# Layer 1 in units of one tile with two places for its middle, and layer 2's first weight scaled by halves

## The chip, the cores and the metric

The kernel runs on one core of one Trainium2 chip. The metric is device time in microseconds (us) of one execution; smaller is better. The core has TensorE (PE, matmuls; PEld are its weight loads), VectorE (DVE), ScalarE (ACT), GpSimd (POOL), SyncE (SP, which issues the DMAs here) and 16 DMA engines.

## What is computed

Masked attention, then two layers of the same shape, on 1536 tokens (2 batches of 768) of width 512:

```python
q_assign = argmax(q_n @ c_n.T)           # 16 clusters per head, k likewise
scores = where(q_assign[:, None] == k_assign[None, :], q @ k.T / 8, -1e9)
x = softmax(scores) @ v                  # 2 batches, 8 heads, 768 x 64, then (1536, 512)
h = x @ w_in; x = (h * cos(h)) @ w_out   # layer 1: 512 -> 2048 -> 512
h = x @ w2_in; out = (h * sigmoid(h)) @ w2_out   # layer 2, same sizes
```

The weights come as 64-bit floats.

## The kernel before

Every product is made of float16 halves: each operand is scaled by a power of two and split into a high and a low part, and three products (high by high, high by low, low by high) are summed in PSUM. So a weight is first unpacked from 64 bits to float32 (`conv`, L685 to L720: three VectorE passes per chunk of 128 x 512, or two and an addition on GpSimd), then a scale is found, then it is split (`split`, L752).

A tile is 128 tokens of one batch, six to a batch. The two batches are cut into `UNITS` (L26) of one or two tiles: one, one, two, two, and then two, two, two. For every unit `attention` (L884) makes, for each tile and each of eight heads, the scores (L905, 128 x 768 in PSUM), their maximum (L915), two one-column factors (L919, L920), the exponential (L934), the halves of it (L941, L948), their transposition by DMA (L514), and the product with V (L958). Eight heads give x of the tile, which is scaled, halved and transposed by DMA into `xT` (L986).

Layer 1 follows a unit later. `layer1_in` (L1011) multiplies the transposed x by the first weight, 768 columns of PSUM at a time (L1034 to L1036), and takes h cos(h) by L1049 to L1058 into `gT`, in halves. `gT` holds one unit: one place in `p_g`. `layer1_out` (L1064) multiplies `gT` by the second weight (L1092 to L1094) in two passes of two blocks of 128 output columns, for there is one PSUM bank (`g2_ps`) of 512 columns, evicts them with a factor (L1099), takes the absolute maximum (L1103, by L411), and stores them to DRAM (L1107). With two tiles in a unit a matmul streams 256 columns, with one 128.

`layer2` (L1116) runs on blocks of 512 tokens. After the last attention and the last conversion of its second weight (`t_swap`) the memory of attention is given to it. It unpacks its first weight (L1128, 16 chunks, each with a sum of squares, L438), finds one scale for it from the sum over all of them (`f_scale`, L1130), splits it in eight pieces (L1140), then splits the second weight (L1151), whose float32 form lies in DRAM. For a block it finds a scale from the maxima of its units (L1169 to L1184), halves the block's x in one operation each (L1185, L1187), multiplies (L1205 to L1207), takes h sigmoid(h) by Tanh (L1215 to L1221), and multiplies by the second weight (L1236 to L1238).

What sets the order: the program is a graph of tasks. `Graph.run` (L141) goes through it once in Python before anything is issued, keeps a clock for each engine from costs written in the code, and starts at each moment the ready task with the smallest due time (`pri`) whose buffers are free. The order that comes out is the order of instructions on each engine. The due times are sums of the unit's number times 1000 and the constants in `T` (L22). They aren't times, only an order. The load of a weight chunk has its own due time, `pri - T["W_AHEAD"]` (L692). Two rules hold the stages in a fixed order: scores of unit u wait for the layer-1 matmuls of unit u - 2 (`g1_dep`, L889 and L912), and those of u wait for the last scores of u + 1 (`last_s`, L1039); likewise the exponentials and the sines (L936, L1053), so that ScalarE seldom changes its table.

In the first stage places are shared: the two halves of `xT` are staging for half of the chunks of layer 1's second weight (`p_wx`, L807 and L846), so the first x wait for all of these (`x_free`, L847 and L988). The four quarters d of that weight are staged in `gT` and in the weight's own memory (`place`, L831); d = 3 goes where d = 1 was. Their due times are `PW_OUT + PW_STEP * d`, plus the chunk (L840), which is 833 for d = 3.

```python
UNITS = [(0, 0, 1), (0, 1, 1), (0, 2, 2), (0, 4, 2), (1, 0, 2), (1, 2, 2), (1, 4, 2)]   # batch, first tile, tiles
p_x, p_g = BufPool(xT), BufPool([gT])
tms.append(add("PE", mm(n, 12), f_mm, [*xready[u], *wdep, *(last_s.get(u + 1, []) ...)], pr + i, acq=[hb], use=[xb]))
t_sc = [f_scale(0, mx0, ms, base), f_scale(1, w2_mx, w2_done, base)]
tx = add("DVE", dve(2048), lambda sx=sx: DV.scalar_tensor_tensor(
    l2["x"][:, 1], l2["xf"], sx, l2["x"][:, 0], op0=ALU.mult, op1=ALU.subtract), [th], pr, use=[xfb, xb], port=True)
```

## Time and profile before

| what | value |
|---|---|
| median of 3 runs | 816.58 us (813.89 to 818.96) |
| the profiled execution, its own time | 815.3 us |
| its span, first to last instruction | 813.6 us |
| busy: TensorE / its weight loads | 709.3 us (87%) / 483.4 us (59%) |
| busy: VectorE / ScalarE / GpSimd | 547.6 / 491.9 / 288.0 us |
| mean granted TensorE clock | 0.979 of 2.4 GHz |
| matmuls | 6744 |

Durations come from the profiled execution. Busy time is the union of an engine's instructions; a matmul's own time includes its way through the array, so the rate is read from the starts of consecutive ones. "Idle before, releaser" is the time an engine stood still ahead of an instruction, and what ended it.

### The profile page before, as it was taken

Reading aid. Unit: us, or ns where it says so; the run is one execution under the profiler, and the core shown is the slowest. Engines: PE = TensorE matmul, PEld = TensorE weight load, DVE = VectorE, ACT = ScalarE, POOL = GpSimd, SP = SyncE. Lnnn points to the kernel's source line nnn. Section 1 sums busy time; section 2 is a strip of 40 time slices with the busy share of each in tenths; the row PEclk is TensorE's granted clock in tenths of the full one; section 3 lists DMA queues with packets and bytes.
Section 4 is the critical chain, followed back from the end, with each engine's and each line's share of the span. In section 5 each row is a group of like instructions: output and inputs, shape, how many; then the busy total and the mean of one; then the engine's idle time right before and its main releaser. Section 6 shows DMA issues by size and latency. Waiting matters only on the chain.

```text
span 813.6 us, 16849 instructions
## 1 busy us (share of the span) xinstructions
PE 709.3 (87%) x6744; PEld 483.4 (59%) x6744; DVE 547.6 (67%) x1143; ACT 491.9 (60%) x767; POOL 288.0 (35%) x239
## 2 busy tenths in 40 slices
PE   2467767988879998998999999975999999999998
PEld 1344344867758876877887888862444444444443
DVE  7899988888887899698688665859860155005500
ACT  4658777788878788698488663836750155015400
POOL 3242466366675457367358540514210000000000
PEclk9999999999998999999999999996999999999999
DMA  8944399989999989959929965331401000000000
GB/s 298 308 163 143 93 222 221 218 137 192 218 184 195 255 156 188 202 134 197 212 90 199 225 194 175 105 130 53 137 27 69 27 1 0 27 27 1 0 27 26
DMA packets 233902, 111.29 MB, mean 137 GB/s; under 512 B 199520, under 2 KB 221536, under 8 KB 233824
## 3 DMA queue, kind: packets, MB, share of 16 engines
q1 hardware_dynamic: 233824, 110.23, 61.4%
q8 instruction: 52, 0.85, 0.4%
q14 instruction: 26, 0.21, 0.1%
HBM read 50.36 MB, written 10.49 MB: 75 GB/s over the span
## 4 chain that ended last, share of the span: by engine, by line
PE 41%; DVE 7%; DMA 5%; issue 2%; POOL 2%; ACT 2%; SPq 1%; POOLq 0%; DVEq 0%; ACTq 0%
PE pb L1206 5%; PE pb L1207 5%; PE pb L1205 5%; DMA gen<-gen 3%; PE xn_ps L1236 3%; PE xn_ps L1238 3%; PE g_ps L1236 3%; PE xn_ps L1237 3%; PE g_ps L1237 3%; PE g_ps L1238 3%; PE g_ps L1094 2%; PE g_ps L1093 2%; PE g_ps L1092 2%; DMA ws<-in_moe_w_in_dram 2%; POOL gen L948 1%
## 5 line engine op out<-in xcount | busy, mean ns | idle before, releaser
L948 POOL TENSOR_TENSOR gen<-e,gen 128x768 f16<-128x768 f32 x96 | 159.0, 1667 | 55.2 <-ACT gen L941 29.3
L1034 PE MATMUL pb<-xT,w 128*128 128x256 f16 (+1 forms) x448 | 111.0, 261 | 3.0 <-ACT e L934 2.7
L1092 PE MATMUL g_ps<-gT,w 128*128 128x256 f16 (+1 forms) x448 | 110.9, 259 | 2.7 <-ACT x2s L1099 2.7
L934 ACT ACTIVATE e<-pb,small 128x768 f32<-128x768 f32 x96 | 94.5, 990 | 27.6 <-DVE small L919 11.6
L1035 PE MATMUL pb<-xT,w 128*128 128x256 f16 (+1 forms) x448 | 111.0, 261 | 0.0
L1093 PE MATMUL g_ps<-gT,w 128*128 128x256 f16 (+1 forms) x448 | 110.9, 259 | 0.0
L1094 PE MATMUL g_ps<-gT,w 128*128 128x256 f16 (+1 forms) x448 | 110.9, 259 | 0.0
L1036 PE MATMUL pb<-xT,w 128*128 128x256 f16 (+1 forms) x448 | 110.8, 261 | 0.0
L915 DVE TENSOR_REDUCE small<-pb 128x1 f32<-128x768 f32 x96 | 89.7, 951 | 11.7 <-PE pb L905 11.0
L1217 DVE SCALAR_TENSOR_TENSOR e<-e,pb 128x512 f32<-128x512 f32 x48 | 32.7, 685 | 95.9 <-ACT e L1215 95.9
L1058 POOL TENSOR_TENSOR gT<-e,gT 128x768 f16<-128x768 f32 (+2 forms) x36 | 56.0, 1559 | 93.3 <-ACT gT L1057 86.2
L905 PE MATMUL pb<-kst,qst 96*128 96x512 f16 (+3 forms) x384 | 78.6, 333 | 9.5 <-ACT e L934 3.2
L958 PE MATMUL xn_ps<-vst,gen 128*128 128x64 f16 x1728 | 66.3, 195 | 21.5 <-DMA gen<-gen 20.6
L958 PEld LDWEIGHTS <-gen 128*128 128x128 f16 x1728 | 60.2, 99 | 34.2 <-DMA gen<-gen 28.9
L1206 PE MATMUL pb<-x2T,w 128*128 128x512 f16 x192 | 73.7, 384 | 6.5 <-DVE x2T L1187 6.5
L1205 PE MATMUL pb<-x2T,w 128*128 128x512 f16 x192 | 73.8, 385 | 3.7 <-ACT x2T L1185 3.7
L1207 PE MATMUL pb<-x2T,w 128*128 128x512 f16 x192 | 73.8, 384 | 0.0
L941 ACT ACTIVATE gen<-e 128x768 f16<-128x768 f32 x89 | 73.1, 841 | 0.2
L905 PEld LDWEIGHTS <-qst 128*128 128x128 f16 (+1 forms) x384 | 35.7, 99 | 29.7 <-issue 13.3
L1221 DVE SCALAR_TENSOR_TENSOR w<-e,w 128x512 f16<-128x512 f32 x48 | 33.8, 708 | 24.6 <-ACT w L1219 24.3
L1215 ACT ACTIVATE e<-pb,cols 128x512 f32<-128x512 f32 x48 | 32.9, 684 | 28.1 <-PE pb L1207 28.1
L1092 PEld LDWEIGHTS <-w 128*128 128x128 f16 x448 | 44.1, 98 | 9.0 <-issue 0.6
(201 smaller groups left out, 1539.4 us busy)
## 6 DMA issues: line engine op xcount, KB each, us to landing
ws<-in_moe_w_out_dram SPq DMA_DIRECT2D x24, 512.0 KB, 4.7
gT<-in_moe_w_in_dram SPq DMA_DIRECT2D x16, 512.0 KB, 5.7
ws<-in_moe_w_in_dram SPq DMA_DIRECT2D x16, 512.0 KB, 4.4
xT<-in_moe_w_out_dram SPq DMA_DIRECT2D x8, 512.0 KB, 4.9
w_dram<-x2s SPq DMA_DIRECT2D x16, 256.0 KB, 2.8
st<-w_dram SPq DMA_DIRECT2D x8, 512.0 KB, 3.8
stq<-in_q_dram SPq DMA_DIRECT2D x6, 512.0 KB, 5.1
gen<-in_k_dram SPq DMA_DIRECT2D x8, 384.0 KB, 5.2
```

The lines of the kernel that those rows point to most:

```text
L905: PE.matmul(out=sbk.ap[:, c0:c1], lhsT=qs.ap[:kk, a, h], rhs=kb.ap[:kk, a, j].rearrange("p t c -> p (t c)")[:, c0:c1], start=(a == 1), sto ...
L948: tl = add("POOL", pool2(S), lambda hi=hi, lo=lo, ex=ex: PO.tensor_tensor(lo(), ex(), hi(), op=ALU.subtract), [th], pr + T["LO"], use=[*eu ...
L958: PE.matmul(out=o, lhsT=hb.ap[:, pi, kt], rhs=vb.ap[:, vi, j, kt], start=(kt == 0 and pi == 0 and vi == 0), stop=(kt == NT - 1 and pi == 1 ...
L1034: PE.matmul(out=o, lhsT=wh[:, d, fs], rhs=xb.ap[:, 0, d, :n], start=(d == 0), stop=False)
L1035: PE.matmul(out=o, lhsT=wh[:, d, fs], rhs=xb.ap[:, 1, d, :n], start=False, stop=False)
L1036: PE.matmul(out=o, lhsT=wl[:, d, fs], rhs=xb.ap[:, 0, d, :n], start=False, stop=(d == ND - 1))
L1092: PE.matmul(out=o, lhsT=wh, rhs=gh, start=(f == 0 and i == 0), stop=False, skip_group_check=True)
L1093: PE.matmul(out=o, lhsT=wh, rhs=gl, start=False, stop=False, skip_group_check=True)
L1094: PE.matmul(out=o, lhsT=wl, rhs=gh, start=False, stop=(f == NF - 1), skip_group_check=True)
L1205: PE.matmul(out=o, lhsT=wh[:, d, fs], rhs=x[:, 0, d], start=(d == 0), stop=False)
L1206: PE.matmul(out=o, lhsT=wh[:, d, fs], rhs=x[:, 1, d], start=False, stop=False)
L1207: PE.matmul(out=o, lhsT=wl[:, d, fs], rhs=x[:, 0, d], start=False, stop=(d == ND - 1))
```

## The change

All layer-1 units have one tile. `GROUP` gives to each unit the number of the old unit it was part of, and the rules that hold the stages in order go by groups; layer 1 of a group's tiles is put into the graph after the attention of the next group. `BASE` takes the place of u * 1000 in the due times. `gT` becomes two places of one tile each and `xT` four. The output of layer 1 is made in one pass of four blocks of 128 columns in the one bank, with four evictions, one maximum and one store per tile. Quarter d = 0 is staged in the first place of `gT`, d = 1 and then d = 3 in the second; the first tile's g waits for d = 0 alone, the second's for d = 1 and d = 3.

In layer 2 the first weight is unpacked so that the columns of f < 8 of all rows come first, and each half has a scale of its own; the second weight's factor is adapted by `so`. A block's x is halved in two pieces, and each matmul group of twelve is cut into two tasks of six, which wait for one piece each. The scale factors of a block become tasks that wait only for what they need.

All constants in `T` differ, so that the order of all engines is another one.

```diff
-T = dict(PW_IN=-24521, PW_OUT=-778, PW_STEP=537, W_AHEAD=-3139, KV0=502, KSTEP0=-8482, V0=2122, Q0=-1625, KSTEP=-1911,
-         PREP=-1178, PREPQ=1263, LD=-18051, ...
+T = dict(PW_IN=-9408, PW_OUT=-7829, PW_STEP=3144, W_AHEAD=-12945, KV0=-16072, KSTEP0=5179, V0=-8782, Q0=-6688,
+         KSTEP=-19233, PREP=-38155, PREPQ=-16289, LD=-5480, ...
-UNITS = [(0, 0, 1), (0, 1, 1), (0, 2, 2), (0, 4, 2), (1, 0, 2), (1, 2, 2), (1, 4, 2)]
+UNITS = [(b, t, 1) for b in range(2) for t in range(6)]
+GROUP = (0, 1, 2, 2, 3, 3, 4, 4, 5, 5, 6, 6)
+BASE = (0, 1000, 2000, 2500, 3000, 3500, 4000, 4500, 5000, 5500, 6000, 6500)
...
-        p_x, p_g = BufPool(xT), BufPool([gT])
+        p_x = BufPool([x[:, z] for x in xT for z in range(2)])
+        p_g = BufPool([gT[:, :, z * NF * P:(z + 1) * NF * P] for z in range(2)])
...
-            g_free.extend(after)
+            g_free[0].extend(w1_out_ready[0, 0] + w1_out_ready[0, 1])
+            g_free[1].extend(after + w1_out_ready[3, 0] + w1_out_ready[3, 1])
...
-            g1_dep = last_mm.get(u - 2, [])
+            gr = GROUP[u]
+            g1_dep = last_mm.get(gr - 2, [])
...
-            for dp in range(ND // 2):
...
+            ob, x2b = Buf(p_g2ps), Buf(p_x2s)
+            prev = []
+            for f in range(NF):
...
+                    for d in range(ND):
+                        o = ob.ap[:, d * n:(d + 1) * n]
...
+                wdep = [t for d in range(ND) for t in w1_out_ready[d, f // 8]]
+                prev = [add("PE", mm(n, 12), f_mm, [gready[u][f * n // EW], *wdep, *prev], BASE[u] + 1000 + T["G2"] + f, acq=[ob], use=[gb])]
+            te = [add("ACT", act(n, SRC), lambda d=d: AC.activation(
+                out=x2b.ap[:, d * n:(d + 1) * n], in_=ob.ap[:, d * n:(d + 1) * n], func=AF.Copy, scale=fac[d]),
...
-            for i in range(NW):
+            for n in range(NW):
+                i = (n % 8) // 2 * 4 + n // 8 * 2 + n % 2
...
-            t_sc = [f_scale(0, mx0, ms, base), f_scale(1, w2_mx, w2_done, base)]
+            t_sc = [f_scale(0, mx0[:, 0:8], ms[0], base), f_scale(1, mx0[:, 8:16], ms[1], base + 50), f_scale(2, w2_mx, w2_done, base)]
...
+            def f_so():
+                DV.tensor_tensor(big, inv[0], inv[1], op=ALU.max)
+                DV.reciprocal(rec, big)
+                for z in range(2):
+                    DV.tensor_scalar(so[z], s[2], inv[z], rec, op0=ALU.mult, op1=ALU.mult)
+                DV.tensor_scalar(iout, inv[2], big, None, op0=ALU.mult)
...
+                for z in range(2):
+                    zs = slice(2 * z, 2 * z + 2)
+                    th = add("ACT", act(1024, SCL), lambda sx=sx, zs=zs: AC.activation(out=l2["x"][:, 0, zs], in_=l2["xf"][:, zs], func=AF.Copy, scale=sx),
+                             [tl, ts, th], pr + z, acq=[] if z else [xb], use=[xfb, xb])
+                    tx.append(add("DVE", dve(1024) + 0.06, lambda sx=sx, zs=zs: DV.scalar_tensor_tensor(
+                        l2["x"][:, 1, zs], l2["xf"][:, zs], sx, l2["x"][:, 0, zs], op0=ALU.mult, op1=ALU.subtract), [th], pr + z, use=[xfb, xb], port=True))
...
+                        for z in range(2):
+                            t = add("PE", mm(N2, 6), lambda z=z, f_mm=f_mm: f_mm(z), [t, tx[z], *[ready[0, 2 * d + (f0 + i) // 8] for d in (2 * z, 2 * z + 1)]],
+                                    pf + i, acq=[] if z or i else [hb], use=[xb, hb])
```

## Rows read from the trace of the kernel before

**Rows 1.** Stretches: length, busy PE, PEld, DVE, ACT, POOL; clock, DMA share, GB/s.
```profile
0.00:75.00 75.00, 36.55 (x306) 25.01 (x307) 65.13 (x160) 45.10 (x59) 24.57 (x55) 1.00 0.72 239
75.00:150.00 75.00, 57.70 (x673) 36.25 (x672) 66.61 (x189) 57.00 (x91) 40.28 (x35) 0.95 0.84 173
...
305.00:375.00 70.00, 65.28 (x810) 53.11 (x807) 59.62 (x128) 59.60 (x101) 41.68 (x28) 0.98 0.98 178
375.00:440.00 65.00, 60.51 (x729) 50.70 (x727) 49.42 (x92) 47.60 (x78) 36.90 (x25) 1.00 0.88 169
...
470.00:545.00 75.00, 73.28 (x671) 65.31 (x669) 50.22 (x80) 40.39 (x74) 21.22 (x15) 1.00 0.50 159
545.00:559.00 14.00, 1.18 (x4) 0.40 (x4) 12.81 (x40) 12.01 (x13) 7.87 (x5) 0.68 0.06 20
```

**Rows 2.** Chain of waits, 540 to 560 us: start, us, engine and line.
```profile
545.28 0.46 ACT x2s L1099
...
551.53 1.73 DVE cols L407
...
556.47 2.27 DVE x2T L1187
```

**Rows 3.** TensorE's timeline around the hole and at the end: start, duration, what.
```profile
544.59 0.27 PE L1094 MATMUL g_ps<-gT,w 128*128 128x256 f16 x1
...
558.78 0.59 PE L1206 MATMUL pb<-x2T,w 128*128 128x512 f16 x1 [6.48 <-DVE x2T L1187]
...
563.75 0.38 PE L1206 MATMUL pb<-x2T,w 128*128 128x512 f16 x1
...
809.37 0.38 PE L1238 MATMUL xn_ps<-w,w 128*128 128x512 f16 x1
```

**Rows 4.** One line's instructions: the loads of 64-bit weights, L692.
```profile
L692 SPq DMA_DIRECT2D ws<-in_moe_w_in_dram x16: 327/328/439, 474.5 to 538.2; - x16
...
DMA to landing us min/median/max: 3.3/4.8/9.2
```

**Rows 5.** VectorE's timeline after the hole: low halves of weight pieces.
```profile
558.65 8.03 DVE L765 SCALAR_TENSOR_TENSOR w<-w,cols 128x1024 f16<-128x1024 f32 x6
```

**Rows 6.** TensorE's timeline, layer 1: a run of narrow and one of wide matmuls.
```profile
152.83 0.22 PE L1034 MATMUL pb<-xT,w 128*128 128x128 f16 x1
...
154.11 0.22 PE L1036 MATMUL pb<-xT,w 128*128 128x128 f16 x1
...
246.31 0.27 PE L1034 MATMUL pb<-xT,w 128*128 128x256 f16 x1
...
247.83 0.27 PE L1036 MATMUL pb<-xT,w 128*128 128x256 f16 x1
```

**Rows 7.** Groups by line and shape: count, busy us, mean ns, idle before and releaser.
```profile
L1092 PE MATMUL g_ps<-gT,w 128*128 128x256 f16 x320 | 87.2, 272 | 2.6 <-ACT x2s L1099 2.6
...
L1057 ACT ACTIVATE gT<-e 128x768 f16<-128x768 f32 x29 | 24.3, 838 | 7.1 <-DVE e L1055 6.9
...
L698 DVE TENSOR_SCALAR pb<-gT 128x512 int32<-128x512 int32 x16 | 11.0, 692 | 3.2 <-DMA gT<-in_moe_w_in_dram 3.0
...
L1099 ACT ACTIVATE x2s<-g_ps,cols 128x256 f32<-128x256 f32 x20 | 8.3, 469 | 6.8 <-PE g_ps L1094 6.8
...
L1052 ACT ACT_TABLE_LOAD x6 | 7.7, 1283 | 0.1
...
L1099 ACT ACTIVATE x2s<-g_ps,cols 128x128 f32<-128x128 f32 x8 | 2.5, 359 | 0.0
```

**Rows 8.** VectorE's timeline, 119 to 160 us.
```profile
130.57 0.69 DVE L713 SCALAR_TENSOR_TENSOR gT<-xT,pb 128x512 int32<-128x512 int32 x1
...
135.55 0.94 DVE L915 TENSOR_REDUCE small<-pb 128x1 f32<-128x768 f32 x1
...
158.98 0.95 DVE L915 TENSOR_REDUCE small<-pb 128x1 f32<-128x768 f32 x1
```

**Rows 9.** SyncE's timeline: the first transposition of x.
```profile
131.69 2.15 SPq L986 DMA_TRANSPOSE xT<-e  x1
```

More of the change, by code (lines that the diff above doesn't have):

```diff
@@ L34 @@
 GRAM_K, GRAM_Q = (0, 0), (0, 0)
[L36 removed]
+IN_PSUM = ((),) * 12
 LO_PE = (4,4)
@@ L329, in fused_kernel @@
         eb_ = [sb([P, EW], F32, f"e{i}") for i in range(NE)]
-        xT = [sb([P, 2, ND, 256], F16, f"xT{i}") for i in range(2)]
+        xT = [sb([P, 2, 2, ND, P], F16, f"xT{i}") for i in range(2)]
         gT = sb([P, 2, NF * 256], F16, "gT")
@@ L681, in x_scale @@
             u = next(i for i, x in enumerate(UNITS) if x[0] == b)
-            xs_task[b] = add("DVE", 0.3, f, [sready[b, hp] for hp in range(NPAIR)], u * 1000)
+            xs_task[b] = add("DVE", 0.3, f, [sready[b, hp] for hp in range(NPAIR)], BASE[u])
         def conv(dst, acc, src, shape3, pri, dst_buf=None, pool=None, deps=(), dst_deps=(), add_low=False, via=False):
@@ L987, in attention @@
                     out=xb.ap.rearrange("p a d n -> p (a d) n")[:, :, ti * P:(ti + 1) * P], in_=xhl().rearrange("p a c -> p (a c)")),
-                    [tx, *(x_free if u in WX and u < 2 else [])], pr, acq=[xb], use=[xs], lat=DLAT, table="x")
+                    [tx, *(x_free if u // 2 in WX and u < 4 else [])], pr, acq=[xb], use=[xs], lat=DLAT, table="x")
                 xready[u].append(tx)
@@ L1102, in layer1_out, with f_mm @@
-            mx2 = col(2)
-            tms = [add("DVE", dve(2 * n), lambda i=i: absmax(mx2[:, i:i + 1], x2b[i].ap[:, :2 * n], AX.X), te[2 * i:2 * i + 2], pr + T["XD"], use=[x2b[i]])
-                   for i in range(2)]
-            tmx = add("DVE", 0.07, lambda: DV.tensor_tensor(mx, mx2[:, 0:1], mx2[:, 1:2], op=ALU.max), tms, pr + T["XD"], port=True)
+            ob, x2b = Buf(p_g2ps), Buf(p_x2s)
+            prev = []
+            for f in range(NF):
+                def f_mm(f=f):
+                    gh = gb.ap[:, 0, f * n:(f + 1) * n]
+                    gl = gb.ap[:, 1, f * n:(f + 1) * n]
+                    for d in range(ND):
+                        o = ob.ap[:, d * n:(d + 1) * n]
+                        wh, wl = w1o_ap[d][:, 0, f], w1o_ap[d][:, 1, f]
+                        PE.matmul(out=o, lhsT=wh, rhs=gh, start=(f == 0 and d == 0), stop=False, skip_group_check=True)
+                        PE.matmul(out=o, lhsT=wh, rhs=gl, start=False, stop=False, skip_group_check=True)
+                        PE.matmul(out=o, lhsT=wl, rhs=gh, start=False, stop=(f == NF - 1), skip_group_check=True)
+                wdep = [t for d in range(ND) for t in w1_out_ready[d, f // 8]]
+                prev = [add("PE", mm(n, 12), f_mm, [gready[u][f * n // EW], *wdep, *prev], BASE[u] + 1000 + T["G2"] + f, acq=[ob], use=[gb])]
@@ L1106, in layer1_out @@
+            te = [add("ACT", act(n, SRC), lambda d=d: AC.activation(
+                out=x2b.ap[:, d * n:(d + 1) * n], in_=ob.ap[:, d * n:(d + 1) * n], func=AF.Copy, scale=fac[d]),
+                [tf, *prev, *(x_free if u == 0 and 2 in WX else [])], pr, acq=[x2b], use=[ob]) for d in range(ND)]
+            tmx = add("DVE", dve(ND * n), lambda: absmax(mx, x2b.ap, AX.X), te, pr + T["XD"], use=[x2b])
             c0 = (b * NT + t0) * P
-            tds = [add("SP", dma(P * 2 * n * 4), lambda i=i: SP.dma_start(
-                out=x2_dram[:, 2 * i:2 * i + 2, c0:c0 + n], in_=x2b[i].ap[:, :2 * n].rearrange("p (d n) -> p d n", d=2)),
-                te[2 * i:2 * i + 2], pr, use=[x2b[i]], lat=SLAT) for i in range(2)]
+            tds = [add("SP", dma(P * ND * n * 4), lambda: SP.dma_start(
+                out=x2_dram[:, :, c0:c0 + n], in_=x2b.ap.rearrange("p (d n) -> p d n", d=ND)), te, pr, use=[x2b], lat=SLAT)]
@@ L1119, in layer2 @@
             l2["swap"] = t_swap
-            s, inv = [col(), col()], [col(), col()]
+            s, inv = [col() for _ in range(3)], [col() for _ in range(3)]
             ready = {}
@@ L1203, in f_mm @@
                             o = hb.ap[:, i * N2:(i + 1) * N2]
-                            for d in range(ND):
+                            for d in (2 * z, 2 * z + 1):
                                 PE.matmul(out=o, lhsT=wh[:, d, fs], rhs=x[:, 0, d], start=(d == 0), stop=False)
@@ L1214, in layer2 @@
                     e = pf - 90
-                    t = add("ACT", act(W, SRC + SCL), lambda rr=rr, ph=ph, ths=ths: AC.activation(out=rr(), in_=ph(), func=AF.Tanh, scale=ths),
-                            tms, e, acq=[rb], use=[hb], table="sin")
+                    t = add("ACT", act(W, SRC + SCL), lambda rr=rr, ph=ph, ths=ths, f0=f0: AC.activation(out=rr(), in_=ph(), func=AF.Tanh, scale=ths[f0 // 8]),
+                            [*tms, tf[f0 // 8]], e, acq=[rb], use=[hb], table="sin")
                     t = add("DVE", dve(W), lambda rr=rr, ph=ph: DV.scalar_tensor_tensor(
@@ L1264, in fused_kernel @@
             attention(u)
-            for w in ([u - 1] if u else []) + ([u] if u == len(UNITS) - 1 else []):
-                G.tag = f'g1_{w}'
-                layer1_in(w)
-                G.tag = f'g2_{w}'
-                layer1_out(w)
+            if u + 1 == len(UNITS) or GROUP[u + 1] != GROUP[u]:
+                for w in [w for w in range(len(UNITS)) if GROUP[w] == GROUP[u] - 1 or GROUP[w] == GROUP[u] == GROUP[-1]]:
+                    G.tag = f'g1_{w}'
+                    layer1_in(w)
+                    G.tag = f'g2_{w}'
+                    layer1_out(w)
         G.tag = 'w2c'
```

116 lines of the change are left out of this document (43 added, 73 removed).

## The prediction, made before the changed kernel was run

> **What bounds the kernel now.** I read the stages first, one row of busy times per stretch [rows 1]. Up to 150 us VectorE sets the pace: 65.1 and 66.6 of 75 us busy, TensorE 36.6 and 57.7. It unpacks the 64-bit weights there and takes the maxima of the first heads. From 305 to 440 us the load is shared: TensorE 65.3 of 70 and 60.5 of 65 us, VectorE 59.6 and 49.4. From 470 to 545 us TensorE is the bound, with 73.3 of 75 us. Then come 14 us in which it does 1.2 us of work, at a granted clock of 0.68. After that it is never idle until the output.
>
> The hole at 545 us is the clearest thing in the trace, so I read the chain of waits through it next [rows 2]. The reader is to see that no single long wait makes it. The last eviction of layer 1 ends at 545.7, the last load of layer 2's first weight being issued at 538.2 [rows 4]; then VectorE works through a string of one-column scale operations (one takes 1.73 us, though it handles 128 numbers) and spends 2.27 us on the low half of a whole 512-token x. Only then, at 558.78, do the multiplications run on. TensorE's own timeline gives the size [rows 3]: the last multiplication of layer 1 ends at 544.59 + 0.27 = 544.86, so 13.9 us are lost. From 558.78 the matmuls are spaced as at half clock: 12 intervals to 563.75 take 4.97 us. From 563.75 to 809.37 there are 1138 intervals of 0.2158 us, so 12 should take 2.59; the clock, down at 1.2 GHz after the hole, costs another 2.4 us.
>
> **The change part by part.** The sum is made against the profiled execution, 815.3 us (span 813.6); the median of the runs shown is 816.58, 0.16% above it.
>
> *The hole.* Layer 2's first weight is now unpacked in the order that completes the columns of f < 8 first, with a scale of their own. Loads run from 474.5 to 538.2 us for 16 chunks [rows 4], 4.2 us each, so eight are in by about 508 and unpacked by about 511. The first x block holds tiles 0 to 3, finished long before. Its scale, both its halves and the first four weight pieces thus have some 30 us in which VectorE is 50.2 of 75 us busy and ScalarE 40.4 [rows 1]. TensorE goes from layer 1 into layer 2 without the hole: -13.9 us, and -2.4 us since the clock has no reason to fall. Ends: nothing gained if the first half comes no earlier, all 16.3 if it does.
>
> *What is late next.* The second half of the weight, still unpacked at about 545, then scaled and split in four pieces. TensorE needs it after 8 x 12 matmuls of 0.2158 us, 20.7 us after it began, so about 566. Six low halves of such pieces take 8.03 us today [rows 5]; four would take 5.4, and with a scale worked out ahead of them be done by about 556. But VectorE then also does the evictions of layer 2. I put +2.0 us for that; between 0 and +9.4 (half the hole back, 7.0, and a clock dip of 2.4).
>
> *Narrow matmuls.* All of layer 1 now streams 128 columns instead of 256 in five of seven units. Both widths are in the trace [rows 6]: 23 intervals from 152.83 to 154.11 make 55.7 ns, 14 intervals from 246.31 to 247.83 make 108.6 ns. Two narrow ones cost 111.3, so 2.7 ns more. Five units have 2 x 192 wide matmuls each, 1920: +5.2 us of TensorE. 671 matmuls lie in the stretch from 470 to 545 us that TensorE bounds [rows 1], +1.8 us whole; of the other 3.4 I take half, because TensorE is some 93% busy from 305 to 440: +3.5, between 1.8 and 5.2.
>
> *Two places for g.* A place now serves one tile, so the next tile may be written while the last one is read. That was hardly a wait: ScalarE's writes into gT of full width came after 7.1 us of idle time in all, 6.9 of it for VectorE's product ahead of them, none for TensorE's reads [rows 7]. I give it nothing; 0 to -7.1.
>
> *Output in one pass.* 14 passes become 12. Between passes TensorE waited 2.6 us for the eviction of the only bank [rows 7]; half of it goes with the other tile's work in between: -1.3 (0 to -2.6). Evictions become 48 of 128 columns, 48 x 0.359 = 17.2 us, where 8.3 + 2.5 = 10.8 us were spent [rows 7]. These +6.4 us lie on ScalarE beside TensorE's work, at 54% load in the last stretch: nothing, at most +6.4 if each held up the next pass.
>
> *The order.* All due times of the planner differ. In the new ones the first Q and K/V pairs come ahead of the first weight's loads, so VectorE and ScalarE need not start on weights alone. What can be got: VectorE's waits for the loads of w_in, 3.0 us [rows 7], when there is something else to do. I take that, -3.0. Ends: all of VectorE's idle time to 150 us, 9.9 + 8.4 = 18.3 us; on the other side the delay of the slower rival below, 17.5.
>
> Sum: -13.9 - 2.4 + 2.0 + 3.5 - 1.3 - 3.0 = -15.1, so 815.3 - 15.1 = 800.2. Against the median it would be 801.5; I say 801.
>
> **The rivals.** *Better packed throughout, 790 us.* Single tiles and the new order let half of VectorE's 18.3 us go, 6.2 beyond the 3.0 counted, and half of TensorE's idle time from 305 to 440 us, (4.7 + 4.5)/2 = 4.6. 801 - 10.8 = 790. For it: engines with much spare time side by side in those rows. Against it: the order of groups is kept (scores of the next group, then layer 1 of this one), so the chain that links them stays.
>
> *Half the hole stays, 808 us.* The second half of the weight is late and TensorE stops inside layer 2's first block: 801 + 7.0 + 2.4 - 2.0. For it: in rows 2 VectorE's small operations run far over their usual length just there. Against it: some 10 us of slack, worked out above.
>
> *Slower: the first x comes late, 822 us.* The transposed x of tile 0 goes to a place where half of layer 1's second weight is staged, so it waits for the unpacking of all of it. Today that ends with the operation at 130.57, and the x goes at 131.69 [rows 8, 9]. The fourth quarter's due time was 833, ahead of tile 1's heads (1000 on); it becomes 1603, behind them, and its loads get a later due time still. The last maximum of tile 1 starts at 135.55. If the quarter runs only after them, four unpackings of three passes of 0.69 us (8.3) and a load of 4.8 [rows 4] put x at about 149 instead of 131.7: +17.5 us, and layer 1, the third group's scores and all that follows hang on it. Then the 3.0 isn't gained either: 801 + 3.0 + 17.5 = 821.5. It decides when the third group's first maximum, at 158.98 today [rows 8], comes more than 15 us later; beyond that the change loses. Against it: the planner may start a later task when VectorE is free, whatever the due time.
>
> *Tables, 805 us.* Six loads of ScalarE's tables stand before a Sin, of 1.28 us each [rows 7]. Layer 2 can now be started while layer 1 runs; if its Tanh falls between the last tile's three Sin operations, up to six more loads are made, 7.7 us, of which half may show: 801 + 3.9. Against it: layer 2's due times lie behind all of layer 1, and 20 us of output matmuls separate the last Sin from the first Tanh. The Trainium skill (ScalarE: Activation LUTs, "Table sets: the hidden batching unit") advises batching calls by table set, not by function, and this change is free to break that; the trace agrees on the price, 1.28 us a load, and shows no case of Tanh amid Sin. By that page's 2.66 us for a whole switch, an estimate, the six would be 16 us.
>
> **How the numbers follow.** Chances: forecast 0.48, better packed 0.21, half the hole 0.14, late x 0.14, tables 0.03. The forecast's own range is 794 to 808. About 1% (808.4 and 824.7, around the median) is what a measurement of this kernel tells from no change. Faster: 0.46 of the forecast, all of better packed, 0.05 of half the hole, 0.02 of tables: 0.74. Slower: 0.08 of late x, where the next groups lose more. Same: the rest, 0.18. The range runs from 784, where better packed gets a half more, to 818, short of most of late x; some 0.15 to 0.2 is left out.
>
> **What would show it.** Right, if TensorE has no gap of over 2 us between its last layer-1 and first layer-2 matmul and the clock stays at full there; if layer 2 starts at about 545 us and its first block has no stop after eight f; if narrow matmuls stay at 55.7 ns; if the third group's first maximum lies near 156 us. The step on the order is wrong if that maximum moves by over 10 us; the one on the hole if layer 1's end and layer 2's start are still apart. The whole is wrong if layer 1 ends much before or after 545 us.

## The result

| | the changed kernel | the kernel before, same chip |
|---|---|---|
| median | 824.53 us (821.44 to 831.25) | 817.77 us (813.89 to 819.45) |
| ratio, 95% interval | 1.0111 [1.0071, 1.015] | |
| profiled execution | 824.31 us, span 822.6 | 815.3 us, span 813.6 |
| matmuls | 8665 | 6744 |

Slower by 1.1%, where 801 was forecast: outside the range. The stretches of the changed kernel (columns as in [rows 1]):

```profile
0.00:75.00 75.00, 37.57 (x371) 28.37 (x371) 63.69 (x180) 50.58 (x67) 19.45 (x53) 1.00 0.69 222
75.00:150.00 75.00, 61.66 (x566) 36.66 (x566) 61.85 (x153) 53.27 (x84) 51.18 (x50) 0.93 0.88 193
...
305.00:375.00 70.00, 64.73 (x1118) 59.22 (x1115) 54.70 (x118) 52.19 (x87) 43.32 (x39) 0.96 0.90 156
375.00:440.00 65.00, 59.42 (x1102) 54.79 (x1100) 45.39 (x83) 48.48 (x82) 36.16 (x30) 1.00 0.97 178
470.00:545.00 75.00, 71.31 (x1325) 70.85 (x1321) 47.96 (x74) 44.54 (x80) 22.68 (x16) 1.00 0.67 179
545.00:559.00 14.00, 12.88 (x232) 12.76 (x230) 9.67 (x23) 7.04 (x14) 7.67 (x6) 1.00 0.44 139
```

The last row answers to the hole: TensorE busy 12.88 of 14 us at full clock, before 1.18 at 0.68 [rows 1]. But what it does there is still layer 1. Its timeline (start, duration, what) shows that the hole is gone and that layer 1 ends at 565.3 us instead of 544.9:

```profile
564.98 0.22 PE L1091 MATMUL g_ps<-gT,w 128*128 128x128 f16 x1
565.04 0.22 PE L1092 MATMUL g_ps<-gT,w 128*128 128x128 f16 x1
565.09 0.38 PE L1210 MATMUL pb<-x2T,w 128*128 128x512 f16 x1
...
818.34 0.38 PE L1247 MATMUL xn_ps<-w,w 128*128 128x512 f16 x1
```

So the miss of 24 us falls into two parts. Layer 1 was to end at 544.9 + 3.5 - 1.3 - 3.0 = 544.1 and ends 21.2 later. From there to the last matmul were 264.5 us before [rows 3], were to be 14.3 less, 250.2, and are 818.34 - 565.26 = 253.1: 2.9 too many.

Where layer 1 lost its time shows in two rows for each kernel: the probabilities-times-V multiplications (`xn_ps<-vst,gen`; first and last start at the end of the numbers) and layer 1's output (`g_ps<-gT,w`). First before, then after:

```profile
L958 PE MATMUL xn_ps<-vst,gen x1728: 189/193/242, 98.6 to 468.0; 128*128 128x64 f16 x192
...
L1094 PE MATMUL g_ps<-gT,w x448: 217/272/314, 158.9 to 544.6; 128*128 128x256 f16 x107, 128*128 128x128 f16 x43
```

```profile
L960 PE MATMUL xn_ps<-vst,gen x1728: 189/193/262, 75.3 to 487.1; 128*128 128x64 f16 x192
...
L1092 PE MATMUL g_ps<-gT,w x768: 217/219/315, 158.1 to 565.0; 128*128 128x128 f16 x192
```

Attention starts 23 us earlier and ends 19 us later; what is left of layer 1 behind it grows by little over 1 us (from 544.9 - 468.2 = 76.7 to 565.3 - 487.3 = 78.0). The loss is in the rounds of heads between 160 and 487 us, and there while scores are made: from the first score multiplication of a group to its last, groups 3 to 6 took 34.4, 35.6, 31.1 and 32.0 us before and take 41.5, 38.8, 34.1 and 33.9, which is some 15 of the 19 us. The granted clock there was the first suspect: 0.93 from 150 to 400 us, before 0.97.

The 2.9 us of layer 2 come from a wait that the prediction had not. Before, all three scales of x were made in the hole ([rows 2] shows one step of one of them, L407; these steps start at 548.19, 551.53 and 554.59). Now the third block's maximum is a matmul (L436) queued on TensorE behind the second block's output; VectorE stands for it, the block's x is halved after it, and TensorE stands in turn (in brackets: idle time, releaser):

```profile
731.81 0.38 PE L1247 MATMUL xn_ps<-w,w 128*128 128x512 f16 x1
732.02 0.22 PE L436 MATMUL pb<-dmax,ones 128*128 128x128 bf16 x1
734.57 0.38 PE L1210 MATMUL pb<-x2T,w 128*128 128x512 f16 x1 [2.33 <-ACT x2T L1190]
...
732.28 0.29 DVE L416 TENSOR_REDUCE cols<-pb 128x1 f32<-128x128 f32 x1 [38.64 <-PE pb L436]
```

### The profile page after: what moved, and what is told of

Same layout as the page of the kernel before. It is cut to its first block, busy times and chain, and to the rows that moved or that the text cites. A ratio compares the mean times of both kernels' runs of the same rounds, so it can differ in the third digit from the quotient of the medians.

```text
span 822.6 us, 20727 instructions
## 1 busy us (share of the span) xinstructions
PE 724.6 (88%) x8665; PEld 521.3 (63%) x8665; DVE 525.9 (64%) x1116; ACT 501.0 (61%) x800; POOL 304.5 (37%) x287
## 4 chain that ended last, share of the span: by engine, by line
PE 45%; DVE 19%; DMA 16%; issue 7%; ACT 6%; POOL 5%; SPq 1%; POOLq 0%; DVEq 0%; ACTq 0%
DMA gen<-gen 8%; PE pb L1211 5%; PE pb L1210 5%; PE pb L1212 5%; POOL gen L950 3%; PE pb L907 3%; DMA ws<-in_moe_w_in_dram 3%; DVE small L917 3%; PE xn_ps L960 3%; PE xn_ps L1247 3%; PE g_ps L1247 3%; PE g_ps L1245 3%; PE xn_ps L1246 3%; PE xn_ps L1245 3%; PE g_ps L1246 3%
## 5 line engine op out<-in xcount | busy, mean ns | idle before, releaser
L1090 PE MATMUL g_ps<-gT,w 128*128 128x128 f16 x768 | 134.9, 221 | 1.1 <-ACT x2s L1096 1.1
L1091 PE MATMUL g_ps<-gT,w 128*128 128x128 f16 x768 | 134.9, 221 | 0.2 <-POOL gT L1060 0.2
L1092 PE MATMUL g_ps<-gT,w 128*128 128x128 f16 x768 | 134.9, 221 | 0.0
L1036 PE MATMUL pb<-xT,w 128*128 128x128 f16 x768 | 132.8, 221 | 1.9 <-DVE w L718 1.4
L1037 PE MATMUL pb<-xT,w 128*128 128x128 f16 x768 | 132.8, 221 | 0.0
L1038 PE MATMUL pb<-xT,w 128*128 128x128 f16 x768 | 132.7, 221 | 0.0
L907 PE MATMUL pb<-kst,qst 96*128 96x512 f16 (+3 forms) x384 | 83.3, 351 | 10.7 <-ACT e L936 5.5
L960 PE MATMUL xn_ps<-vst,gen 128*128 128x64 f16 x1728 | 67.5, 198 | 24.7 <-DMA gen<-gen 24.5
L1060 POOL TENSOR_TENSOR gT<-e,gT 128x768 f16<-128x768 f32 (+1 forms) x36 | 53.5, 1489 | 81.8 <-ACT gT L1059 65.5
L1090 PEld LDWEIGHTS <-w 128*128 128x128 f16 x768 | 76.0, 99 | 4.5 <-issue 0.3
L943 ACT ACTIVATE gen<-e 128x768 f16<-128x768 f32 x96 | 78.3, 840 | 0.3 <-DMA gen<-gen 0.2
L1037 PEld LDWEIGHTS <-w 128*128 128x128 f16 x768 | 75.8, 99 | 2.2 <-issue 2.2
L1091 PEld LDWEIGHTS <-w 128*128 128x128 f16 x768 | 76.0, 99 | 1.7 <-issue 1.2
L1092 PEld LDWEIGHTS <-w 128*128 128x128 f16 x768 | 76.0, 99 | 0.3 <-issue 0.3
L1036 PEld LDWEIGHTS <-w 128*128 128x128 f16 x768 | 75.8, 99 | 0.3 <-issue 0.3
L1038 PEld LDWEIGHTS <-w 128*128 128x128 f16 x768 | 75.8, 99 | 0.0
L1210 PE MATMUL pb<-x2T,w 128*128 128x512 f16 x192 | 72.8, 379 | 3.1 <-ACT x2T L1190 2.3
L1211 PE MATMUL pb<-x2T,w 128*128 128x512 f16 x192 | 72.8, 379 | 0.9 <-DVE x2T L1192 0.9
```

The source lines that it names most:

```text
L907: PE.matmul(out=sbk.ap[:, c0:c1], lhsT=qs.ap[:kk, a, h], rhs=kb.ap[:kk, a, j].rearrange("p t c -> p (t c)")[:, c0:c1], start=(a == 1), sto ...
L960: PE.matmul(out=o, lhsT=hb.ap[:, pi, kt], rhs=vb.ap[:, vi, j, kt], start=(kt == 0 and pi == 0 and vi == 0), stop=(kt == NT - 1 and pi == 1 ...
L1036: PE.matmul(out=o, lhsT=wh[:, d, fs], rhs=xb.ap[:, 0, d, :n], start=(d == 0), stop=False)
L1037: PE.matmul(out=o, lhsT=wh[:, d, fs], rhs=xb.ap[:, 1, d, :n], start=False, stop=False)
L1038: PE.matmul(out=o, lhsT=wl[:, d, fs], rhs=xb.ap[:, 0, d, :n], start=False, stop=(d == ND - 1))
L1090: PE.matmul(out=o, lhsT=wh, rhs=gh, start=(f == 0 and d == 0), stop=False, skip_group_check=True)
```

## The experiments

Times are medians, ratios are against the kernel before run beside it on the same chip. "End of layer 1" and "end of attention" are read from the two rows above, with a matmul's length added.

**The parts of the change alone.**

*l2_halves_only*: the kernel before with the changed `layer2` (and `NKEEP` 320).

```diff
-            t_sc = [f_scale(0, mx0, ms, base), f_scale(1, w2_mx, w2_done, base)]
+            t_sc = [f_scale(0, mx0[:, 0:8], ms[0], base), f_scale(1, mx0[:, 8:16], ms[1], base + 50), f_scale(2, w2_mx, w2_done, base)]
```

> Layer 1 and all due times as before; only layer 2 is changed (weight in halves, x in two pieces). Theory 1 (layer 2's part closes the hole and keeps its gain of 13.9 + 2.4 us; the loss lies in layer 1): layer 1 ends at 545 us as before, the hole is under 2 us, ratio to before 0.978 to 0.985. Rival (the hole was worth less, because layer 2's first block then waits for the second half): ratio above 0.99.

Measured: 808.05 us, ratio 0.991 [0.988, 0.994]. That is on the rival's side, narrowly, and half of what theory 1 asked. From layer 1's end to the last matmul it takes 257.5 us, before 264.5. The hole is closed, but TensorE stops 3 us in the first block, for a bank of its output memory that an unpacking of the weight's second half holds between two of its passes, and again at the third block:

```profile
543.97 0.38 PE L1219 MATMUL pb<-x2T,w 128*128 128x512 f16 x1
547.28 0.38 PE L1217 MATMUL pb<-x2T,w 128*128 128x512 f16 x1 [2.94 <-DVE w L713]
...
712.16 0.22 PE L431 MATMUL pb<-dmax,ones 128*128 128x128 bf16 x1
714.72 0.38 PE L1217 MATMUL pb<-x2T,w 128*128 128x512 f16 x1 [2.34 <-ACT x2T L1197]
```

*narrow*: the kernel before, each matmul of 256 columns in layer 1 as two of 128.

```diff
-                            PE.matmul(out=o, lhsT=wh[:, d, fs], rhs=xb.ap[:, 0, d, :n], start=(d == 0), stop=False)
+                            for c in range(0, n, P):
+                                PE.matmul(out=o[:, c:c + P], lhsT=wh[:, d, fs], rhs=xb.ap[:, 0, d, c:c + P], start=(d == 0), stop=False)
```

(in `f_mm` of both parts of layer 1, for all three products)

> The kernel before, every layer-1 matmul of 256 columns issued as two of 128 with the same weights; order, units and everything else untouched. Theory 1 (narrow matmuls cost 2.7 ns a pair and lie mostly on TensorE's path): 3.5 to 5.2 us more, ratio 1.004 to 1.0065. Rival a (they are hidden): ratio within 0.001 of 1. Rival b (twice the weight loads and instructions slow TensorE by more than the rows of narrow matmuls show): over 8 us, ratio above 1.010.

Measured: 822.82 us, 1.0091 [1.0057, 1.0124]. That lies between theory 1 and rival b, and the interval reaches into both. Layer 1 ends at 552.2, 7.3 us later. Behind the end of attention (473.6 instead of 468.2) the cost is 78.6 - 76.7 = 1.9 us, as worked out; 5.4 arise in the rounds, where 1.7 were allowed. (Attention in the old order ended between 465.4 and 468.2 in other runs, so some 2 us of the 5.4 may be chance.)

*old_units_new_due* and *units_old_due*: the constants `T` exchanged between the kernels, so that new due times order the old units, and old ones the new units.

```diff
-T = dict(PW_IN=-24521, PW_OUT=-778, PW_STEP=537, W_AHEAD=-3139, KV0=502, KSTEP0=-8482, V0=2122, Q0=-1625, KSTEP=-1911,
+T = dict(PW_IN=-9408, PW_OUT=-7829, PW_STEP=3144, W_AHEAD=-12945, KV0=-16072, KSTEP0=5179, V0=-8782, Q0=-6688,
...
```

> The kernel before with the due times of the changed kernel: old units, one place, old layer 2. Theory 2 (the new order costs the time, whatever the units): slower than the changed kernel's own loss in layer 1, layer 1 ends after 560 us, ratio above 1.02, and the half-clock time between 150 and 350 us is above 25 us where before has 13.6. Rival (one-tile units cost it, the order does not): ratio within 0.01 of 1.

> The changed kernel with the old due times. Theory 2 (the new order costs the time): layer 1 ends near 550 us, and with the hole closed the time is below the kernel before, ratio 0.985 to 0.995. Rival (one-tile units cost it): layer 1 ends after 565 us, ratio 1.01 or more.

Measured: 834.13 us (1.0251 [1.0205, 1.0297]) and 842.2 us (1.0335 [1.0299, 1.0371]); layer 1 ends at 559.9 and 583.4. With the old units theory 2 holds: the new due times alone put layer 1's end 15.0 us later.

```profile
L1094 PE MATMUL g_ps<-gT,w x448: 217/272/417, 155.4 to 559.7; 128*128 128x256 f16 x107, 128*128 128x128 f16 x43
```

The scores of groups 3 and 4 take 40.7 and 43.3 us there (34.4 and 35.6 before), and the granted clock from 150 to 350 us is 0.94 (0.97 before). With the new units the rival holds: the old due times are worse still.

*units_old_l2*: the changed kernel with the whole old `layer2`.

```diff
-            t_sc = [f_scale(0, mx0[:, 0:8], ms[0], base), f_scale(1, mx0[:, 8:16], ms[1], base + 50), f_scale(2, w2_mx, w2_done, base)]
+            t_sc = [f_scale(0, mx0, ms, base), f_scale(1, w2_mx, w2_done, base)]
...
```

> The changed kernel with layer 2 as it was before (one scale for the whole first weight), so units of one tile, two places, one pass and the new due times alone. Theory (the parts add up: layer 2's halves give what l2_halves_only gave, 6.6 us, and the loss lies in layer 1): layer 1 ends near 565, a hole of some 10 to 14 us comes back behind it with a fall of the clock, and the time is about 831 to 836, a ratio of 1.016 to 1.022. Rival (the new due times had already moved the first weight's loads and unpacking, so the halves add nothing): 824 to 827, within 2 us of the changed kernel.

Measured: 836.54 us, 1.0275 [1.0243, 1.0307]; layer 1 ends at 563.2 and the hole is back. The theory holds in kind, but the parts don't simply add up: layer 2's halves gain 12.0 us here, 6.6 in the old order. Beside old_units_new_due, which also has the new due times and the old layer 2, the new units cost 2.4 us more, less than the noise. So of the 18.3 us that layer 1 comes late here, the due times bring 15.0 with the old units already.

**Why the rounds are slower.**

*after_warm*: TensorE is kept busy where it waited (`npv` counts the heads).

```diff
+WARM = {16: 12, 18: 40, 28: 64, 34: 13, 36: 38, 37: 55, 45: 19, 47: 25}
...
+                        for _ in range(WARM.get(npv[0], 0)):
+                            PE.matmul(out=o, lhsT=ident, rhs=ident[:, :D], start=True, stop=True, skip_group_check=True)
+                        npv[0] += 1
```

> The changed kernel with 266 matmuls of 64 columns on the identity put ahead of the eight pairs of probabilities-times-V multiplications that stood waiting for transposed probabilities between 175 and 280 us (12, 40, 64, 13, 38, 55, 19 and 25 of them; their results are overwritten by the real ones). They fill waits of 0.5 to 2.7 us and so keep TensorE busy. Theory (the waits make TensorE's clock fall, and the half clock of 34.1 us between 150 and 400 us is what the layer-1 stage lost): half clock there falls below 18 us, the last layer-1 matmul ends 6 to 10 us earlier than 565.3, and the time falls by 6 to 10 us to about 815 to 818. Rival 1 (the dips are only a sign: VectorE or the transpositions set the pace): half clock falls but the end stays within 2 us. Rival 2 (the filling matmuls themselves delay what waits): the time rises by up to 266 x 0.028 = 7.4 us.

Measured: 824.51 us, 1.0121 [1.0097, 1.0145]: the same as without. From 150 to 400 us the clock is back at 0.97, yet layer 1 ends at 564.8, 0.5 us earlier. The falls of the clock were a sign of the waits and not what set the pace: rival 1. (That the filling matmuls took back what the clock gave, rival 2, this run can't exclude by itself; the next one speaks against it.) The rows are for the kernel before, the changed one and this one:

```profile
150.00:400.00 250.00, 222.79 (x3133) 186.32 (x3130) 213.54 (x475) 202.55 (x331) 144.69 (x99) 0.97 1.05 190
```

```profile
150.00:400.00 250.00, 221.10 (x3738) 194.62 (x3739) 197.42 (x439) 198.44 (x329) 148.78 (x124) 0.93 0.99 174
```

```profile
150.00:400.00 250.00, 221.77 (x3997) 196.90 (x3993) 194.91 (x425) 197.55 (x327) 147.98 (x123) 0.97 0.97 174
```

*after_thin*: a third of layer 1's matmuls left out, those with the weights' low halves.

```diff
-                            PE.matmul(out=o, lhsT=wl[:, d, fs], rhs=xb.ap[:, 0, d, :n], start=False, stop=(d == ND - 1))
```

> The changed kernel without layer 1's products with the weights' low halves: a third of layer 1's matmuls, 1536 of 4608, are left out, 1536 x 0.0557 = 86 us of TensorE, 60 us of it ahead of the last probabilities-times-V multiplication. The order of all other instructions stays. Theory 1 (TensorE's work sets the pace of the rounds, so narrow matmuls and clock are the loss): that multiplication comes 45 to 60 us before 487.3. Theory 2 (the heads set the pace while scores run, TensorE only between them): the stretches of scores of groups 3 to 6, 41.5, 38.8, 34.1 and 33.9 us, fall by less than 3 us each, the stretches between them by about a third, and the last multiplication comes 20 to 35 us earlier.

Measured: 815.97 us, 1.0012 [0.9973, 1.005]. 86 us less work of TensorE give 8.6 us. Attention ends at 478.4, 8.9 us earlier, less than either theory asked:

```profile
L960 PE MATMUL xn_ps<-vst,gen x1728: 190/193/261, 74.9 to 478.2; 128*128 128x64 f16 x192
```

The stretches of scores of groups 3 to 6 (first score to last) become 38.8, 36.8, 35.4 and 35.1 us, and those between them, 40.4, 33.6 and 34.2 us, become 40.6, 31.3 and 31.1. (Layer 1 ends at 550.7, 14.6 us earlier; layer 2 loses 6.3 of that again.) TensorE, by its matmuls the busiest of the compute engines in these rounds, doesn't pace them. The Trainium skill (Perfetto Trace Analysis, "Identifying the Most-Contended Engine") advises optimizing the engine with the highest occupancy first, and judges TensorE by the busy share of its weight loads or by its rate of work, not by its matmuls' busy time. By weight loads and occupancy the changed kernel's row above singles out no engine: weight loads 194.62, VectorE 197.42, ScalarE 198.44 of 250 us.

So the head's own chain was looked at. Matching the n-th instruction of each kind in the trace gives, per head, the time from its last score matmul's end to its first probabilities-times-V matmul; medians in us:

| group | before | changed | of these: exponential's end to copy's end, before / changed |
|---|---|---|---|
| 2 | 17.5 | 19.5 | 3.6 / 5.1 |
| 3 | 21.4 | 24.8 | 3.6 / 5.1 |
| 4 | 17.8 | 24.1 | 2.8 / 5.3 |
| 5 | 18.2 | 22.5 | 3.5 / 4.4 |
| 6 | 18.6 | 19.0 | 4.4 / 3.9 |

*after_cast_moved* and *halves_cast_moved*: the high-half copy on VectorE, at the same place of the order. (The expectation's 21.5 us for group 2 is the mean; the median is 19.5.)

```diff
-                    th = add("ACT", act(S, SRC if here else 0.0), lambda hi=hi, ex=ex: AC.activation(out=hi(), in_=ex(), func=AF.Copy), [te],
+                    th = add("ACT", act(S, SRC if here else 0.0), lambda hi=hi, ex=ex, u=u: DV.tensor_copy(hi(), ex()) if 2 <= GROUP[u] <= 5 else AC.activation(out=hi(), in_=ex(), func=AF.Copy), [te],
```

> The changed kernel with the first half-precision copy of a head's probabilities made on VectorE instead of ScalarE in groups 2 to 5 (64 of 96 heads), at the same place of the order; every other engine's instructions stay as they are. In the changed kernel a head of those groups takes 21.5 to 24.8 us (medians) from its scores to its first probabilities-times-V multiplication, before 17.5 to 21.4; the copy waits 4.5 us on average behind other ScalarE work, before 2.9. Theory (ScalarE's queue makes the heads slow, and slow heads make the rounds long): the medians fall by 2 us or more, the last probabilities-times-V multiplication comes 6 to 14 us before the 487.3 us of the changed kernel, and the time is 811 to 819. Rival (the heads wait for the transpositions or for TensorE anyway): the medians stay within 1 us, and the time within 3 us of 824. Rival 2 (64 x 0.565 us more on VectorE delay the maxima): slower, up to 830.

> The same move of the copies to VectorE in groups 2 to 5 in the kernel of before with layer 2's halves. Theory (there ScalarE's queue is short, 2.9 us on average): 808 within 4 us either way; the medians from scores to probabilities-times-V fall by less than 1.5 us. Rival (ScalarE paces the heads there too): 800 to 804.

Measured: 842.52 us (1.0317 [1.026, 1.0374]) and 830.3 us (1.0174 [1.0127, 1.0221]): both 18 to 22 us slower. The copy ends even later after the exponential (6.4 to 7.6 us in the changed order) and the maxima start up to 2.8 us after their scores (medians of a group). VectorE, idle for 36.5 us of these 250 before and 52.6 in the changed kernel, has no time at the right places. The theory on ScalarE's queue falls in this form; rival 2 was right in kind, and too small.

*after_half_T* and *halves_half_T*: half the bytes of the probabilities' transposition, in the changed kernel and in l2_halves_only. The transposition of the high halves is left out, and the low halves are multiplied in their place.

```diff
-                    tt = transpose(lambda hb=hb: hb.ap.rearrange("p a t c -> p (a t) c"), lambda pb_=pb_: pb_.ap.rearrange("p a c -> p (a c)"),
+                    tt = transpose(lambda hb=hb: hb.ap[:, 0], lambda pb_=pb_: pb_.ap[:, 1],
...
-                                PE.matmul(out=o, lhsT=hb.ap[:, pi, kt], rhs=vb.ap[:, vi, j, kt],
+                                PE.matmul(out=o, lhsT=hb.ap[:, 0, kt], rhs=vb.ap[:, vi, j, kt],
```

> The changed kernel with only the low half of each head's probabilities transposed, and multiplied in place of the high half too: the high half's transposition is left out (half the bytes of 96 transpositions), while the order, the waits and the number of matmuls stay. In the chain of waits from 150 to 470 us the transposition of probabilities takes 20.6% in the changed kernel, 8.2% before. Theory (in the changed kernel the rounds are paced by the chain of a head through its transposition, before they mostly were not): the last probabilities-times-V multiplication comes 10 to 20 us before 487.3, layer 1 ends 10 to 20 us before 565.3, and the time is 804 to 814. Rival (the chain only passes there because something has to be last; no single step sets the pace): less than 5 us earlier, 820 or more.

> The same for the kernel of before with layer 2's halves. Theory (before, the transposition was not what paced the rounds): the last probabilities-times-V multiplication comes less than 8 us before 465.4, the time is 800 to 808, so that the two kernels come nearer: their layer-1 ends, 22.6 us apart, less than 14 us. Rival 1 (transpositions set the pace in both): 10 to 20 us earlier here too, 788 to 798, and the distance stays. Rival 2 (in neither): both within 5 us, the distance stays.

Measured: 801.56 us (0.98 [0.9742, 0.9857]) and 796.13 us (0.9765 [0.9735, 0.9795]): 23.0 and 11.9 us less than their counterparts. Landing falls from 4.5 to 2.8 us. Attention ends at 463.7 and 454.0, layer 1 at 541.8 and 531.2: the distance shrinks from 22.6 to 10.6 us. The ends of attention, changed order, then old:

```profile
L960 PE MATMUL xn_ps<-vst,gen x1728: 189/193/261, 74.8 to 463.5; 128*128 128x64 f16 x192
```

```profile
L958 PE MATMUL xn_ps<-vst,gen x1728: 189/193/262, 100.3 to 453.8; 128*128 128x64 f16 x192
```

So the transposition, or what hangs on its bytes, paces the rounds in both kernels (rival 1 in part: 12 us in the old order, where less than 8 was expected), and halving it gained 1.9 times as much in the changed one, more than the theory there asked. What of the halving counts wasn't separated: SyncE also issues a transposition in 1.23 us instead of 1.73 (medians), and the busy share of the DMA engines from 150 to 400 us falls from 0.99 to 0.77. That share was the highest of its row from the start; but with 1.05 it was higher still before, at the shorter time, so it doesn't tell the two orders apart.

The shares of the chain of waits that the expectation of after_half_T compares, 20.6% and 8.2%, can't be set side by side. In the kernel before, the view follows the chain back to 327.8 us only, so its 8.2% of 320 us come from the last 142 of them. From 330 to 470 us the chain is whole in each kernel; its summary by line (cut off at the end by the view itself) before, then changed, then changed with half the bytes:

```profile
by line: DMA gen<-gen 18.7%; POOL gen L948 7.8%; issue 7.3%; PE xn_ps L958 6.6%; SPq L514 4.9%; PE g_ps L1093 4.2%; PE g_ps L1094 4.2%; PE g_ps L1092 4.2%; PE pb L1034 3.9%; PE pb L1035 3.9%; PE pb L1036 3.8%; PE pb L905 3.3%; DVE small L91
```

```profile
by line: DMA gen<-gen 24.0%; POOL gen L950 10.5%; issue 8.3%; DMA qst<-natq 6.9%; PE xn_ps L960 6.5%; SPq L519 4.5%; PE pb L907 3.8%; DMA ws<-in_moe_w_out_dram 3.5%; PE pb L1036 3.4%; PE pb L1038 3.4%; PE pb L1037 3.4%; PE g_ps L1090 2.2%; 
```

```profile
by line: PE xn_ps L960 12.8%; PE pb L907 10.5%; PE pb L1038 8.8%; PE pb L1036 8.7%; PE pb L1037 8.7%; PE g_ps L1090 7.0%; PE g_ps L1092 6.9%; PE g_ps L1091 6.9%; ACT e L936 5.3%; issue 4.5%; DMA w_dram<-x2s 4.1%; ACT e L1054 2.1%; DVE e L10
```

The transposition (`DMA gen<-gen`) heads the list in both orders, with 1.3 times the share in the changed one, and with half its bytes it leaves the head of the list to TensorE.

**Mending it.**

*l2_max_first*, *l2_no_bank* (in the old order) and *after_max_first* (in the changed one): early due times for the second and third block's maximum and scales; in l2_no_bank the unpackings of the second half also no longer use the bank.

```diff
                 pr = base + u2 * 1000
+                pm = pr - 900 if u2 else pr
...
-                t = add("DVE", 0.4, f_m, [x2done[u][0] for u in us], pr)
+                t = add("DVE", 0.4, f_m, [x2done[u][0] for u in us], pm)
...
-                ms[n // 8] += conv(lambda r=r: raw(r), mx0[:, n:n + 1], w_in_src(w2i, i), 0, base + n * 10 - T["W2"], None, p_ws2, [t_swap], add_low=n % 4 < LOW[3], via=n % 4 < VIA[3])
+                ms[n // 8] += conv(lambda r=r: raw(r), mx0[:, n:n + 1], w_in_src(w2i, i), 0, base + n * 10 - T["W2"], None, p_ws2, [t_swap], add_low=n % 4 < LOW[3], via=n < 8 and n % 4 < VIA[3])
```

> The kernel with only layer 2's halves, and the maximum over partitions and the scales of layer 2's second and third block given a due time before the block ahead of them, so that the third block's maximum no longer stands in TensorE's queue behind the second block's output matmuls. Theory (that wait costs what TensorE stood idle at the third block, 2.56 + 1.11 us, a little more if the clock falls there): no gap of over 0.5 us before the third block's first matmuls, and 3.5 to 5 us less than l2_halves_only, so about 803.5 to 804.5 us and a ratio of 0.985 to 0.987 to the kernel before. Rival (the third block waits for the single place of its x or for the low half itself, the scale being ready or not): the gap stays above 2 us and the time stays at 808 +- 1.5.

> The kernel with layer 2's halves and early scales (l2_max_first), in which the unpackings of the second half of layer 2's first weight no longer take a bank of TensorE's output memory as their place between two passes. Theory (TensorE stands 3.1 us at 546 because such an unpacking holds the bank): that stop is gone, the clock doesn't fall after it, and the time is 3 to 5 us less than l2_max_first's 806.5, so 801.5 to 803.5 (ratio about 0.984 to 0.986). Rival (VectorE's work just there is late anyway, and the stop moves to the matmuls that need the second half): 806 +- 1.5.

> The changed kernel with only the due time of the maxima over partitions and scales of layer 2's second and third block moved ahead of the block before them. In the changed kernel there is no stop at the start of layer 2 that could take the gain back, as there was in l2_max_first. Theory (the third block's maximum behind the second block's output matmuls costs its stop, 2.55 + 1.11 us): no stop of over 0.5 us in layer 2, 3 to 5 us less than the changed kernel's 824.5, so 819.5 to 821.5. Rival (the stop moves): 823 to 826.

Measured: 806.46 (0.9897 [0.987, 0.9925]), 806.66 (0.9894 [0.9853, 0.9934]) and 823.01 us (1.0074 [1.0047, 1.0101]). The stop at the third block is gone in all three, and each time some 1.5 of its 3.7 us are gained against the same kernel without the early maximum, with intervals that overlap; leaving the bank alone gives nothing more (806.66 for 806.46). In after_max_first the early maximum now stands among the first block's matmuls at 571.2, and the next of them waits 1.6 us for a bank that an unpacking holds. In l2_max_first the first block's stop stays, and behind it the granted clock falls: 0.83 from 545 to 565 us, where l2_halves_only had 1.00 from 542 to 565. l2_no_bank still stops at 545, 2.6 us, now for the low half of x. VectorE has much to do just there, and the stop moves: the rivals.

*l2_pe_T1* (on l2_max_first) and *after_pe_T* (on the changed kernel): one head of eight in groups 2 to 5 transposed on TensorE.

```diff
-                                   2 * NT, [tl], pr, [hb], [], [pb_], NT * b + t < PET[2])
+                                   2 * NT, [tl], pr, [hb], [], [pb_], 2 <= u <= 5 and h in (7,))
```

> The kernel with layer 2's halves and early scales (l2_max_first), in which one head of eight in groups 2 to 5 (8 of 96) has its probabilities transposed on TensorE through an output bank and copied out by ScalarE or VectorE, instead of by DMA; the planner makes its order anew. Theory (the DMA transposition paces the rounds, and TensorE has time to spare there): 2 to 6 us less than 806.5, so 800 to 804. Rival (the bank, the copy and the new order cost more than the DMA's share gives back, as moving the copies to VectorE did): 810 to 825.

> The changed kernel with one head of eight in groups 2 to 5 transposed on TensorE instead of by DMA, the planner making its order anew (what l2_pe_T1 did to the other order; there layer 1 ended at 545.4, as without it, 544.9). Theory (the transposition paces the changed order more): layer 1 ends 3 to 10 us before 565.3, time 814 to 821. Rival (the new order costs what the DMA gives back, as in l2_pe_T1): layer 1 ends at 565 +- 4, 821 to 829; or the order made anew loses as the one of units_old_due did: over 829.

Measured: 799.97 us (0.9792 [0.9757, 0.9827]), the best version found, and 825.85 us (1.0122 [1.0086, 1.0158]). But l2_pe_T1 isn't faster for the expected reason: its layer 1 ends at 545.4, with DMA's transpositions at 544.9. The gain is in layer 2, from 255.5 to 250.0 us between layer 1's end and the last matmul: in the order made anew the first block stops 1.3 us where it stopped 2.9 us with the clock at half behind it (a matmul of 512 columns 0.59 us). First l2_pe_T1, then l2_max_first:

```profile
545.31 0.38 PE L1218 MATMUL pb<-x2T,w 128*128 128x512 f16 x1
546.94 0.38 PE L1219 MATMUL pb<-x2T,w 128*128 128x512 f16 x1 [1.26 <-DVE x2T L1200]
```

```profile
546.14 0.38 PE L1220 MATMUL pb<-x2T,w 128*128 128x512 f16 x1
549.45 0.59 PE L1218 MATMUL pb<-x2T,w 128*128 128x512 f16 x1 [2.93 <-DVE w L713]
```

In after_pe_T it is the other way round: layer 1 ends at 559.2, 6.1 us earlier, as the theory asked, and new stops in layer 2 (2.6 us at 564.0, 0.9 at 585.1, with the granted clock at 0.96 from 559 to 600 us) take it back: the rival's time.

## Why the prediction was wrong

- *The hole, -13.9, and the clock behind it, -2.4*: right. TensorE goes from layer 1 into layer 2 without a gap and at full clock.
- *Second half late, +2.0*: right in kind, and 1.1 us in the changed kernel (0.7 and 0.4 us of stops up to 573.3). What was missing is the third block's maximum, +3.7: the step "a stall goes, what is late next" looked at the weight alone, and not at the scales that the hole had hidden.
- *Narrow matmuls, +3.5*: the mechanism was right, the term mis-sized: +7.3. The stretch that TensorE bounds cost the 1.8 foreseen; in the rounds "half, because TensorE is some 93% busy" gave 1.7, and 5.4 came (some 2 of them perhaps by chance, as said above).
- *Two places, 0*: not tried by itself. *One pass, -1.3*: the wait for the bank fell from 2.6 to 1.1 us, -1.5, and the 48 evictions take 14.5 us instead of the 17.2 estimated:

```profile
L1090 PE MATMUL g_ps<-gT,w 128*128 128x128 f16 x768 | 134.9, 221 | 1.1 <-ACT x2s L1096 1.1
...
L1096 ACT ACTIVATE x2s<-g_ps,cols 128x128 f32<-128x128 f32 x48 | 14.5, 369 | 8.7 <-PE g_ps L1092 7.5 <-PE pb L427 1.2
```

- *The order, -3.0*: this step failed. It looked for what the order could give up to 150 us and took the rounds behind as they were. The runs showed +15.0 in its place: that much later layer 1 ends when the new due times order the old units (old_units_new_due). VectorE's idle time to 150 us even rose, from 18.3 to 24.5 us (11.3 + 13.2 in the stretches above). Of the 21.2 us that layer 1 came late in the changed kernel, 3.8 are the narrow term, so some 17 are the order's, near the 18.0 between -3.0 and +15.0. The order counts in the rounds, where a head of groups 2 to 6 takes 0.4 to 6.3 us longer from its scores to its product with V. That the longer head is what stretches the rounds is argued, not shown; before the change that time was the thing to read, and only TensorE's busy share was read.
- *The rivals.* The first x isn't late: it goes at 130.82 (before 131.69, [rows 9]), and the third group's first maximum starts at 160.70 (158.98, [rows 8]). So the slower side came, but by another mechanism than the rival's. The sign that was to tell of a wrong order, that maximum moving by over 10 us, didn't come either: it is read at 160 us, ahead of where the time was lost. Only the sign for the whole, layer 1 ending away from 545 us, did. Tables: 6 loads at the exponential and 6 at Sin as before, 1.28 us each.

What stays open: why the changed order leans on the transposition more. A copy that waits longer behind other ScalarE work (4.5 us on average in groups 2 to 5, before 2.9) is part of the longer head, but taking it away from ScalarE by force made things worse, so it isn't shown as the cause. Of the 10.6 us between the two orders that remain with half the bytes, narrow matmuls would be 7.3, if their cost is the same there; that wasn't tried.

## What to carry to other kernels

Where engines pass work round in a fixed order, the busy shares of the compute engines don't tell which step paces it: take work or bytes away from one suspect at a time and see what comes back (86 us of TensorE gave 8.6, half of 96 transpositions gave 23). Before two shares of a chain are compared, see that both chains cover the stretch. A change of the whole order has to be judged by the latency of one item through the loop, in every stretch. And when a hole is closed, list all that was done in it: each of these things now queues behind something.
